# Attention and two feed-forward stages on one core: 1 / row sum spread through a four-row tile that a DMA makes, and the first chunk's sums copied by two engines in turn

## The chip, the core and the metric

The kernel runs on one core of a Trainium2 chip. The core has five engines that each work through their own instructions in order: TensorE (PE, matmuls; PEld in the profile is its loading of stationary operands), VectorE (DVE), ScalarE (ACT), GpSimd (POOL) and SyncE (SP). SP computes nothing here: it issues every DMA of this kernel, one after another, each when its inputs are ready. Engines wait for each other through semaphores. The metric is device time in microseconds, the median of the runs of one kernel.

## What is computed

The reference, cut to its arithmetic (q, k and v hold 2 x 8 heads of 768 x 64; 16 centroids per head; everything is float32):

```python
mask = argmax(q_n . c_n) == argmax(k_n . c_n)          # per head, cluster of each row
scores = where(mask, q @ k.T / sqrt(64), -1e9)
attn = exp(scores - max(scores))
attn = attn / (sum(attn) + 1e-9)
x = (attn @ v)  as [1536, 512]
x = square(relu(x @ w_in)) @ w_out                     # w_in 512 x 2048
p = domain_probs / (sum(domain_probs) + 1e-9)          # 4 experts
out = sum over e of p[:, e] * (relu(x @ w1[e]) @ w2[e])  # w1[e] 512 x 1024
```

## The kernel before

A float32 product is made of three products of float32r parts (high x high, high x low, low x high), so most values exist as a pair such as `hh`, `hl`.

**Attention** is a loop over 96 steps `g` (`NU`: 16 heads of 6 tiles of 128 query rows). In a step the kernel emits the scores of tile g+2 (`emit_S`, tile `s`), their maximum (`emit_max`, DVE), the exponential of tile g+1 with its row sums into `sums` (`emit_exp`, ACT), the transposes of tile g (`emit_T`: PE writes `t`, ACT copies it to `pth`, DVE makes `ptl`), and in turn one half of the product with v for two tiles (`emit_PV`, six matmuls, tile `po`). The table `ORDER` fixes the order inside even and odd steps. Two places of a step, `X1` and `X2`, take work from lists by step: PE's part stands there, and its copy out of PSUM (`Y1`, `Y2`) later in the step. `X1` takes the first piece of the step and `X2` the second. All these pieces share one PSUM buffer, `m` (`ps_m`, one buffer). Such pieces are the transposes of the next heads' k and q (`trans_slot`), the cluster products (`assign_slot`), the transposes of the one-hot cluster rows `oh` (`onehot_slot`, copied to `ohm` by ACT and sent by four DMAs), and the slots of `norm_slots`.

**norm_slots** divides by the row sums, once for each of 8 pairs of heads, numbered 0 to 7 here. After the last `emit_PO` of a pair its slots go into the list `nq`, one for each following step (`None` is a step without a piece). `f1` makes 1 / sum and splits it into two parts, `rs`. `f2` transposes `rs` by a matmul into `m`, ACT copies it to `rt` (24 rows of 128), and POOL adds `xm` to `xs`. `f3(0)` and `f3(1)` spread the values over 128 rows with a constant `sel` of ones and zeros, three matmuls of 128 columns each; ACT copies the result to `rb`, and POOL multiplies by `xs` and splits into `xh`, `xl`. For pair j, `f2` stands in step 12j+17. In step 12j+16 SP is given the loads of the next heads (`load_v`, `load_pair`: `nv`, `nk`, `nq`) and, late in the loop, of pieces of `w_out` (`load_piece`, tile `raw`).

**The last pair** (7) is emitted after the loop, written out by hand: `f1`, a first group of matmuls of the next stage (`early_gemm1(0)`), `f2`, the last products with v, `f3(0)`, `early_gemm1(1)`, `f3(1)`, `early_gemm1(2)` and so on; here ACT and DVE do POOL's part of `f3`.

**The two feed-forward stages** are one loop over 12 chunks `ci` of 512 hidden columns, 3 blocks `tb` of 512 tokens and 4 groups `m` of 128 columns. A step of it emits `gemm1` (12 matmuls, then ACT's relu, square and cast, POOL's `hl`), then the `gemm2` of four steps before (12 matmuls into four PSUM tiles `o0` to `o3`, one buffer each) and then `run_plan`, the splitting of later weights (ACT casts `w0h` or `w1h`, and DVE makes the low part, then five operations on `cva` for the next block). When a block's sum over a chunk is complete, `evac` takes `o0` to `o3` to `acc`: for the first chunk by four ACT copies (line 682), later by DVE adds (line 684).

Of the kernel before, what the change touches and what calls it, by code (L numbers as in the profile page):

```python
# [8 lines left out]
F32 = mybir.dt.float32  # L9
F32R = mybir.dt.float32r  # L10
I32 = mybir.dt.int32
AF = mybir.ActivationFunctionType
ALU = mybir.AluOpType
# [20 lines left out]
def moe_attention_kernel(  # L34
# [13 lines left out]
    nc = tc.nc  # L48
# [5 lines left out]
    B, H, S, D = q.shape  # L54
# [3 lines left out]
    NTT = S // 128  # L58
# [4 lines left out]
    HALF = S // 2  # L63
    QT = HALF // 128
# [5 lines left out]
    const = ctx.enter_context(tc.tile_pool(name="const", bufs=1))  # L70
# [5 lines left out]
    identf = const.tile([128, 128], F32, name="identf")  # L76
    identr = const.tile([128, 128], F32R, name="identr")
    zeros = const.tile([128, 1, 1], F32, name="zeros")
    cc = const.tile([128, H, 2 * C], F32R, name="cc")
    wgt = const.tile([128, 1, C], F32, name="wgt")  # L80
    sel = const.tile([NTT * 4, NTT, 128], F32R, name="sel")
    pe_p = const.tile([128, B * NTT, E], F32, name="pe_p")

    xh = [xpool.tile([128, KD, TB], F32R, name=f"xh{i}") for i in range(NTB)]
# [126 lines left out]
    with tc.manual_schedule():  # L211
# [8 lines left out]
        xs_p = right(actx, "xs", 2)  # L220
        sm_p = right(actx, "sm", 4)
# [53 lines left out]
            nc.gpsimd.memset(wgt[:, :, c:c + 1], float(C - c))  # L275


        idv = identf[0:NTT * 4, 0:NTT * 4].rearrange("p (t h s) -> p t h s", t=NTT, h=2)
        for h in range(2):
            nc.vector.tensor_tensor(  # L280
                sel[:, :, h * D:(h + 1) * D],
                idv[:, :, h, 0:1].to_broadcast([NTT * 4, NTT, D]),
                idv[:, :, h, 1:2].to_broadcast([NTT * 4, NTT, D]), op=ALU.add)

# [283 lines left out]
        def norm_slots(hp, last=False):  # L570
            st = {}
            def f1():
                sm = sums_t.pop(hp)
                r = sm_p.tile([128, 2, NTT], F32, tag="r", name="r", bufs=1)
                rs = st["rs"] = sm_p.tile([128, NTT, 2, 2], F32R, tag="rs", name="rs", bufs=2)
                rv = r.rearrange("p h t -> p t h")
                dq.extend([
                    lambda: nc.vector.tensor_scalar(r, sm, 1e-9, None, op0=ALU.add),
                    lambda: nc.vector.reciprocal(r, r),
                    lambda: nc.vector.tensor_copy(rs[:, :, :, 0], rv),  # L580
                    lambda: nc.vector.tensor_tensor(
                        rs[:, :, :, 1], rv, rs[:, :, :, 0].bitcast(F32), op=ALU.subtract),
                ])

            def f2():
                m = ps_m.tile([NTT * 4, 128], F32R, tag="m", name="m")
                nc.tensor.transpose(m, st["rs"].rearrange("p t h s -> p (t h s)"), identr)

                def evac():
                    rt = st["rt"] = xs_p.tile([NTT * 4, 128], F32R, tag="rt", name="rt")  # L590
                    nc.scalar.copy(rt, m.bitcast(F32))
                    if hp in xm_t:
                        xm = xm_t.pop(hp)
                        nc.gpsimd.tensor_tensor(xs_t[hp], xs_t[hp], xm, op=ALU.add)
                return evac

            def f3(half):
                b, kt = divmod(hp, H // 2)
                m = ps_m.tile([128, HALF], F32, tag="m", name="m")
                for j in range(QT):  # L600
                    nc.tensor.matmul(  # L601
                        m[:, j * 128:(j + 1) * 128], sel[:, half * QT + j], st["rt"],
                        start=True, stop=True)

                def evac():
                    rb = xs_p.tile([128, HALF], F32, tag="rb", name="rb")
                    nc.scalar.copy(rb, m)
                    (nc.vector if last else nc.gpsimd).tensor_tensor(
                        rb, rb, xs_t[hp][:, half * HALF:(half + 1) * HALF], op=ALU.mult)
                    c0 = b * S + half * HALF  # L610
                    col = c0
                    while col < c0 + HALF:
                        tb, o = divmod(col, TB)
                        n = min(TB - o, c0 + HALF - col)
                        xn = rb[:, col - c0:col - c0 + n]
                        hi = xh[tb][:, kt, o:o + n]
                        if last:
                            nc.scalar.copy(hi, xn)
                        else:
                            round_pool(hi, xn)  # L620
                        (nc.vector if last else nc.gpsimd).tensor_tensor(
                            xl[tb][:, kt, o:o + n], xn, hi.bitcast(F32), op=ALU.subtract)
                        col += n
                return evac

            return [f1, None, None, f2, lambda: f3(0), lambda: f3(1)]


        mp = {}
# [2 lines left out]
        o_t = {}  # L632
# [43 lines left out]
        def evac(ci, tb, n):  # L676
            first = ci in (0, NC1)
            last = ci in (NC1 - 1, NCH - 1)
            acc = acc_t[tb][:, n]
            if ci < NC1:  # L680
                if first:
                    nc.scalar.copy(acc, o_t[n])
                else:
                    nc.vector.tensor_tensor(acc, o_t[n], acc, op=ALU.add)
                if last:
# [228 lines left out]
            gemm1(*its[n], ps=s[:, 0])  # L914

        hp, pr = NH // 2 - 1, NU // 2 - 1
        f1, _, _, f2, f3, f4 = norm_slots(hp, last=True)
        f1()
        while dq:
            dq.pop(0)()  # L920
# [70 lines left out]
```

## Time and profile before

| | us |
|---|---|
| median of 2 runs | 1083.69 (1083.56 to 1083.82) |
| the profiled execution's own time | 1085.59 |
| its span, first to last instruction | 1083.8 |
| PE busy | 1055.2 (97%) |
| DVE busy | 503.8 (46%) |
| ACT busy | 431.0 (40%) |
| POOL busy | 326.3 (30%) |

Times in rows are microseconds from the span's start; "L601" is line 601 of the kernel before. A timeline row gives start, duration, engine, line, operation, written tile <- read tiles, shape, count, and in brackets how long the engine had been idle and what it waited for. Matmuls overlap in PE's pipeline, so the distance between two starts tells more than a matmul's duration. A DMA's row on SP is the time that SP spends issuing it; "to landing" counts from the start of the issue until the data is there. PEclk is the granted clock of PE as a share of full speed.

### The profile page before, as it was taken

The page shows a single profiled execution, that of the slowest core. Times are in us where ns is not written, and L with a number is a line of the kernel's source. Part 1 is how long each engine was busy: PE and PEld are TensorE (multiplying, and loading weights), DVE is VectorE, ACT ScalarE, POOL GpSimd, SP SyncE. Part 2 cuts the span into 40 slices and gives each one's busy share as a digit, 9 for nine tenths or more (in the row PEclk, how much of TensorE's full clock was granted, in tenths as well). Part 3 has the DMA queues.
Part 4 walks back from the last instruction along what each step waited for, and adds up shares of the span by engine and source line. Part 5 has one row for each costly group of instructions (what it writes and reads, how often), then busy time and mean ns, then how long its engine had stood idle before and what let it go on. Part 6 is the DMA issues. An engine that isn't in the chain of part 4 may idle for free.

```text
span 1083.8 us, 14176 instructions
## 1 busy us (share of the span) xinstructions
PE 1055.2 (97%) x5457; PEld 901.4 (83%) x5457; DVE 503.8 (46%) x838; ACT 431.0 (40%) x879; POOL 326.3 (30%) x405
## 2 busy tenths in 40 slices
PE   8899999998999999999999999999999999999998
PEld 7889888998887888888888888888888888888886
DVE  8688888787788763821122222222222223222322
ACT  6588887887655543434432121211212111121110
POOL 2457766665222222224534020211202112020000
PEclk9899999999999999999999999999999999999999
DMA  5666666873023230211102011110111102000012
GB/s 153 157 152 141 151 153 159 202 177 93 1 78 117 81 114 10 107 39 39 40 1 78 1 39 39 39 39 1 39 39 40 39 1 78 0 1 1 1 39 78
DMA packets 56978, 74.73 MB, mean 69 GB/s; under 512 B 26576, under 2 KB 32016, under 8 KB 56912
## 3 DMA queue, kind: packets, MB, share of 16 engines
q1 hardware_dynamic: 56912, 73.84, 25.0%
q8 instruction: 43, 0.70, 0.3%
q14 instruction: 23, 0.19, 0.1%
HBM read 43.05 MB, written 3.15 MB: 43 GB/s over the span
## 4 chain that ended last, share of the span: by engine, by line
PE 76%; DVE 3%; ACT 1%; DMA 1%; POOL 1%; issue 1%; SPq 0%; POOLq 0%; ACTq 0%
PE o L671 35%; PE h L641 11%; PE h L643 11%; PE h L642 11%; PE t L522 2%; PE s L489 2%; PE po L538 1%; PE po L536 1%; DVE cva L173 1%; PE m L388 1%; DMA q<-nql 1%; DVE cva L178 0%; PE m L601 0%; ACT p L509 0%; DMA k<-nkh 0%
## 5 line engine op out<-in xcount | busy, mean ns | idle before, releaser
L655 DVE SCALAR_TENSOR_TENSOR hl<-h,hh 128x512 fp32r<-128x512 f32 x96 | 66.4, 692 | 393.4 <-ACT hh L654 393.4
L654 ACT ACTIVATE hh<-h 128x512 fp32r<-128x512 f32 x96 | 57.4, 598 | 429.0 <-PE h L643 429.0
L641 PE MATMUL h<-xh,w0h 128*128 128x512 f32 x560 | 218.0, 389 | 0.0
L642 PE MATMUL h<-xl,w0h 128*128 128x512 f32 x560 | 217.9, 389 | 0.0
L643 PE MATMUL h<-xh,w0l 128*128 128x512 f32 x560 | 217.8, 389 | 0.0
L671 PE MATMUL o<-w1h,hh 128*128 128x512 f32 x384 | 149.4, 389 | 0.0
L671 PE MATMUL o<-w1l,hh 128*128 128x512 f32 x384 | 149.4, 389 | 0.0
L671 PE MATMUL o<-w1h,hl 128*128 128x512 f32 x384 | 149.4, 389 | 0.0
L643 PEld LDWEIGHTS h<-xh,w0l 128*128 128x128 f32 x560 | 105.2, 188 | 22.0
L641 PEld LDWEIGHTS h<-xh,w0h 128*128 128x128 f32 x560 | 105.3, 188 | 21.8
L642 PEld LDWEIGHTS h<-xl,w0h 128*128 128x128 f32 x560 | 105.1, 188 | 21.9
L652 POOL TENSOR_TENSOR hl<-r,hh 128x512 fp32r<-128x512 f32 x48 | 63.3, 1318 | 186.4 <-ACT hh L651 125.0
L528 DVE TENSOR_TENSOR ptl<-t,pth 128x384 fp32r<-128x384 f32 x192 | 99.3, 551 | 28.9 <-ACT pth L527 28.5
L196 POOL TENSOR_TENSOR w0l<-raw,w0h 128x512 fp32r<-128x512 f32 x32 | 41.2, 1289 | 236.7 <-ACT w0h L195 236.7
L498 DVE TENSOR_REDUCE nb<-s 128x1 f32<-128x768 f32 x96 | 91.2, 950 | 16.8 <-PE s L489 15.6
L527 ACT CAST pth<-t 128x384 fp32r<-128x384 f32 x192 | 83.2, 485 | 28.4 <-PE t L522 27.8
L522 PE MATMUL t<-identf,p 128*128 128x128 f32 x576 | 88.1, 280 | 6.2 <-DVE ptl L528 6.0
L489 PE MATMUL s<-k,q 80*128 80x384 f32 (+1 forms) x384 | 87.4, 348 | 3.1 <-DMA k<-ohm 2.7
L509 ACT ACTIVATE p<-s,nb 128x768 f32<-128x768 f32 x96 | 87.4, 911 | 7.0 <-DVE nb L498 6.9
L671 PEld LDWEIGHTS o<-w1l,hh 128*128 128x128 f32 x384 | 72.1, 188 | 15.0
L671 PEld LDWEIGHTS o<-w1h,hh 128*128 128x128 f32 x384 | 72.0, 188 | 15.0
L671 PEld LDWEIGHTS o<-w1h,hl 128*128 128x128 f32 x384 | 72.0, 188 | 15.0
(154 smaller groups left out, 1627.1 us busy)
## 6 DMA issues: line engine op xcount, KB each, us to landing
raw<-in_moe_w_dram SPq DMA_DIRECT2D x16, 1024.0 KB, 5.1
raw<-in_moe_w_in_dram SPq DMA_DIRECT2D x8, 1024.0 KB, 5.1
q<-nqh SPq DMA_DIRECT2D x42, 192.0 KB, 3.0
raw<-in_moe_w_out_dram SPq DMA_DIRECT2D x6, 1024.0 KB, 5.0
k<-nkh SPq DMA_DIRECT2D x28, 192.0 KB, 3.3
q<-nql SPq DMA_DIRECT2D x28, 192.0 KB, 3.8
nv<-in_v_dram SPq DMA_DIRECT2D x16, 192.0 KB, 3.7
out_dram<-acc SPq DMA_DIRECT2D x12, 256.0 KB, 2.1
```

Source lines behind the costliest of these rows:

```text
L489: nc.tensor.matmul(s[:, j, 0:HALF], stk[i, nq][:, t * 128:(t + 1) * 128], stk[i, nk][:, j * HALF:(j + 1) * HALF], start=first, stop=not first)
L498: nc.vector.tensor_reduce(out=nb, in_=s_ps[u][:, :, 0:HALF], axis=AX.XY, op=ALU.max, negate=True)
L509: nc.scalar.activation(p, s_ps.pop(u)[:, :, 0:HALF], AF.Exp, bias=nb_t.pop(u), accum_out=sums_t[hp][:, i % 2, t:t + 1])
L522: nc.tensor.transpose(tp[:, j], p_sb[u][:, half, j * 128:(j + 1) * 128], identf)
L527: return (lambda: nc.scalar.copy(dh, tp), lambda: nc.vector.tensor_tensor(dl, tp, dh.bitcast(F32), op=ALU.subtract))
L528: lambda: nc.vector.tensor_tensor(dl, tp, dh.bitcast(F32), op=ALU.subtract))
L641: nc.tensor.matmul(ps, wh[:, kt, ms], xh[tb][:, kt], start=(kt == 0), stop=False)
L642: nc.tensor.matmul(ps, wh[:, kt, ms], xl[tb][:, kt], start=False, stop=False)
L643: nc.tensor.matmul(ps, wl[:, kt, ms], xh[tb][:, kt], start=False, stop=(kt == KD - 1))
L652: nc.gpsimd.tensor_tensor(hl, r, hh.bitcast(F32), op=ALU.subtract)
L655: nc.vector.scalar_tensor_tensor(out=hl, in0=ps, scalar=0.0, in1=hh.bitcast(F32), op0=ALU.max, op1=ALU.subtract)
L671: nc.tensor.matmul(o_t[n], a, b, start=(ft == 0 and z == 0), stop=(ft == NF - 1 and z == 2))
```

## The change

Two edits.

**1 / sum.** `rs` is laid out with the tile index last, so the transposed `rt` has its 24 rows in the order (head, part, tile). Behind ACT's copy a new DMA on SP turns `rt` into `rw`, 4 rows (head, part) of 768 columns. `sel` shrinks to 4 x 128, and each `f3` is one matmul of 384 columns that reads `rw`. The slots get one more `None`, so `f3(0)` and `f3(1)` move one step later. After the loop, pair 7 keeps its order.

**First chunk's sums.** `o0` and `o2` are still copied by ACT, `o1` and `o3` now by DVE.

```diff
-    sel = const.tile([NTT * 4, NTT, 128], F32R, name="sel")
+    sel = const.tile([4, 128], F32R, name="sel")
...
-                rs = st["rs"] = sm_p.tile([128, NTT, 2, 2], F32R, tag="rs", name="rs", bufs=2)
-                rv = r.rearrange("p h t -> p t h")
+                rs = st["rs"] = sm_p.tile([128, 2, 2, NTT], F32R, tag="rs", name="rs", bufs=2)
+                rv = r
...
                     nc.scalar.copy(rt, m.bitcast(F32))
+                    rw = st["rw"] = xs_p.tile([4, S], F32R, tag="rw", name="rw", bufs=1)
+                    nc.sync.dma_start(
+                        out=rw.bitcast(F32).rearrange("c (t n) -> c t n", t=NTT),
+                        in_=rt.bitcast(F32))
...
-                for j in range(QT):
-                    nc.tensor.matmul(
-                        m[:, j * 128:(j + 1) * 128], sel[:, half * QT + j], st["rt"],
-                        start=True, stop=True)
+                nc.tensor.matmul(
+                    m, sel, st["rw"][:, half * HALF:(half + 1) * HALF], start=True, stop=True)
...
-            return [f1, None, None, f2, lambda: f3(0), lambda: f3(1)]
+            return [f1, None, None, f2, None, lambda: f3(0), lambda: f3(1)]
...
                 if first:
-                    nc.scalar.copy(acc, o_t[n])
+                    if n % 2:
+                        nc.vector.tensor_copy(acc, o_t[n])
+                    else:
+                        nc.scalar.copy(acc, o_t[n])
...
-        f1, _, _, f2, f3, f4 = norm_slots(hp, last=True)
+        f1, _, _, f2, _, f3, f4 = norm_slots(hp, last=True)
```

Where the new DMA stands on SP, first as it was around the normalisation of pair 0 (`nv`, `nk`, `nq` are the loads of later heads, `k` and `q` the stacked operands of a coming head):

```order
L248 DMA nv<-in_v_dram 128x384
L241 DMA nk<-in_k_dram 128x6x64 x2
L241 DMA nq<-in_q_dram 128x6x64 x2
L379 DMA k_1282<-nkh 64x768
L381 DMA k_1282<-nkl 64x768
L379 DMA q_1285<-nqh 64x768
```

and as it is with the change (lines of the changed kernel):

```order
L248 DMA nv<-in_v_dram 128x384
L241 DMA nk<-in_k_dram 128x6x64 x2
L241 DMA nq<-in_q_dram 128x6x64 x2
L592 DMA rw<-rt 4x6x128
L378 DMA k_1271<-nkh 64x768
L380 DMA k_1271<-nkl 64x768
L378 DMA q_1274<-nqh 64x768
```

The DMA stands behind the loads of `nv`, `nk`, `nq` and ahead of the next `k`; for pair 4 two `raw` pieces of 256 KB stand between `nq` and it as well, for pair 5 two such pieces and no `nk`, `nq`, and for pairs 6 and 7 nothing near.

On PE, steps 18 to 20 around the same place before (`t` the transposes, `po` the products with v, `m<-rt,sel` the two `f3`, `m<-identr,oh` the transposes of one-hot rows):

```order
L522 MATMUL t<-identf,p 128x128 x3
L601 MATMUL m<-rt,sel 128x128 x3
L522 MATMUL t<-identf,p 128x128 x3
...
L601 MATMUL m<-rt,sel 128x128 x3
L522 MATMUL t<-identf,p 128x128 x6
...
L448 MATMUL m<-identr,oh 64x128 x3
L522 MATMUL t<-identf,p 128x128 x3
L536 MATMUL po<-pth,vv 128x256
```

and with the change:

```order
L488 MATMUL s<-k_1390,q_1392 128x384 x2
L603 MATMUL m<-rw,sel 128x384
L521 MATMUL t<-identf,p 128x128 x6
...
L447 MATMUL m<-identr,oh 64x128 x3
L521 MATMUL t<-identf,p 128x128 x3
L603 MATMUL m<-rw,sel 128x384
L535 MATMUL po<-pth,vv 128x256
```

`f3(0)` now has the place in step 19 that `f3(1)` had, and `f3(1)` stands in step 20 as a second piece, behind the one-hot transposes, which write the same single buffer `m`.

On DVE, where the first block's sum of the first chunk is taken over, before (one round of weight splitting, and the next):

```order
L173 SCALAR_TENSOR_TENSOR cva<-raw,cva 128x512
L178 SCALAR_TENSOR_TENSOR cva<-raw,cva 128x512
L186 TENSOR_TENSOR w0l<-cva,w0h 128x4x128
L162 TENSOR_SCALAR cva<-raw 128x512
L165 TENSOR_SCALAR cva<-cva 128x512
```

and with the change:

```order
L173 SCALAR_TENSOR_TENSOR cva<-raw,cva 128x512
L178 SCALAR_TENSOR_TENSOR cva<-raw,cva 128x512
L684 COPY acc_4768<-o_4795 128x512
L684 COPY acc_4768<-o_4803 128x512
L186 TENSOR_TENSOR w0l<-cva,w0h 128x4x128
L162 TENSOR_SCALAR cva<-raw 128x512
```

The copies of `o1` and `o3` stand on DVE behind the whole round of splitting that `run_plan` gave it a step before.

## Rows read from the trace of the kernel before

**Rows 1.** Windows of the span by stage: attention, the passage from attention to the feed-forward stages, and the steady feed-forward stages. Columns: length, then busy time and count of PE, PEld, DVE, ACT and POOL, granted clock of PE, share of the DMA engines, GB/s.

```profile
60.00:120.00 60.00, 56.19 (x434) 52.62 (x433) 53.13 (x95) 47.87 (x115) 39.35 (x62) 1.00 0.67 151
300.00:360.00 60.00, 57.80 (x248) 47.37 (x247) 50.87 (x76) 32.02 (x56) 15.27 (x12) 0.97 0.29 91
600.00:800.00 200.00, 200.00 (x884) 165.59 (x883) 48.60 (x72) 33.98 (x61) 30.91 (x24) 1.00 0.10 32
```

**Rows 2.** Timeline of PE, steps 17 to 19 (normalisation of pair 0).

```profile
72.09 0.87 PE L489 MATMUL s<-k,q 128*128 128x384 f32 x4
...
74.23 0.87 PE L489 MATMUL s<-k,q 128*128 128x384 f32 x4
76.45 0.55 PE L522 MATMUL t<-identf,p 128*128 128x128 f32 x3 [1.35 <-DVE ptl L528]
76.93 0.55 PE L601 MATMUL m<-rt,sel 24*128 24x128 f32 x3
...
78.50 0.87 PE L489 MATMUL s<-k,q 128*128 128x384 f32 x4
79.29 0.55 PE L601 MATMUL m<-rt,sel 24*128 24x128 f32 x3
79.77 0.87 PE L522 MATMUL t<-identf,p 128*128 128x128 f32 x6
```

**Rows 3.** Timeline of ACT and SP at the same place: the copy that makes `rt`, the issue of two `nq` loads, the issue after them.

```profile
73.06 0.25 ACT L591 CAST rt<-m 24x128 fp32r<-24x128 f32 x1
...
74.60 2.43 SPq L241 DMA_DIRECT2D nq<-in_q_dram  x2
...
77.07 0.77 SPq L379 DMA_DIRECT2D k<-nkh  x1
```

**Rows 4.** The view of one tile's instructions, for the second of those `nq` loads (issue in ns, its start, then its time to landing) and for the `k` behind it (its time to landing).

```profile
L241 SPq DMA_DIRECT2D nq<-in_q_dram x1: 1739/1739/1739, 75.3 to 75.3; - x1
DMA to landing us min/median/max: 5.1/5.1/5.1
...
DMA to landing us min/median/max: 3.6/3.6/3.6
```

**Rows 5.** The same for pair 4 (PE's `f3(1)`; the `raw` piece that the new DMA will follow and its time to landing) and for pair 5 (the same, two pieces in one answer).

```profile
211.92 0.55 PE L601 MATMUL m<-rt,sel 24*128 24x128 f32 x3
L105 SPq DMA_DIRECT2D raw<-in_moe_w_out_dram x1: 431/431/431, 211.0 to 211.0; - x1
DMA to landing us min/median/max: 5.2/5.2/5.2
244.69 0.55 PE L601 MATMUL m<-rt,sel 24*128 24x128 f32 x3
L105 SPq DMA_DIRECT2D raw<-in_moe_w_out_dram x2: 447/708/969, 239.4 to 240.4; - x2
DMA to landing us min/median/max: 4.7/4.9/5.1
```

**Rows 6.** All 60 DMAs from `ohm` (24 KB each), the view of that tile: time to landing. Then the timeline of step 20 after pair 0: the one-hot transposes into `m`, ACT's copy of it, and PE's next product.

```profile
DMA to landing us min/median/max: 1.9/1.9/3.9
...
82.30 0.37 PE L448 MATMUL m<-identr,oh 128*64 128x128 f32 x3
82.71 0.47 ACT L453 CAST ohm<-m 64x384 fp32r<-64x384 f32 x1
82.77 0.37 PE L536 MATMUL po<-pth,vv 128*128 128x256 f32 x1
```

**Rows 7.** Timeline of PE after pair 4: two waits that the kernel before has there.

```profile
215.36 0.38 PE L448 MATMUL m<-identr,oh 128*64 128x128 f32 x3 [0.34 <-POOL oh L422]
218.16 0.81 PE L388 MATMUL m<-cc,k 128*128 128x32 f32 x6 [0.68 <-DMA k<-nkl]
```

**Rows 8.** Timeline of the last pair (7), after the loop: `rt`, `f3(0)`, the relu after `early_gemm1(1)`, and DVE's part of `f3(1)`.

```profile
293.33 0.25 ACT L591 CAST rt<-m 24x128 fp32r<-24x128 f32 x1
293.63 0.55 PE L601 MATMUL m<-rt,sel 24*128 24x128 f32 x3 [0.62 <-ACT rt L591]
...
297.17 0.60 ACT L649 ACTIVATE r<-s 128x512 f32<-128x512 f32 x1 [1.20 <-PE s L643]
...
299.50 1.37 DVE L608 TENSOR_TENSOR rb<-rb,xs 128x384 f32<-128x384 f32 x1 [3.06 <-ACT rb L607]
```

**Rows 9.** Timeline where the first block's sum is taken over: the end of a `gemm1`, ACT's four copies, PE's wait for the first of them, and the last of DVE's five operations of that round. Then the group of DVE's later adds from the same PSUM tiles, from the view of lines by form (count, then busy us, mean ns).

```profile
327.38 0.39 PE L643 MATMUL h<-xh,w0l 128*128 128x512 f32 x1
329.33 2.04 ACT L682 COPY acc<-o 128x512 f32<-128x512 f32 x4
329.96 0.50 PE L671 MATMUL o<-hh,w1h 128*128 128x512 f32 x1 [2.20 <-ACT acc L682]
331.41 0.69 DVE L178 SCALAR_TENSOR_TENSOR cva<-raw,cva 128x512 int32<-128x512 int32 x1
...
L684 DVE TENSOR_TENSOR acc<-o,acc 128x512 f32<-128x512 f32 x36 | 23.6, 687 | 83.2 <-PE o L671 83.2
```

**Rows 10.** PE around two long waits: a wait in the attention loop, and windows of PE alone (length, busy time and count, granted clock) that begin with the end of it and with the end of the wait of rows 9.

```profile
269.20 0.58 PE L489 MATMUL s<-k,q 80*128 80x384 f32 x2 [2.69 <-DMA k<-ohm]
269.00:274.00 5.00, 4.80 (x26) 0.66 0.00 0
331.00:335.00 4.00, 4.00 (x12) 0.57 0.06 25
```

More of the change, by code (lines that the diff above doesn't have):

```diff
@@ L275, in moe_attention_kernel @@
             nc.gpsimd.memset(wgt[:, :, c:c + 1], float(C - c))
-        idv = identf[0:NTT * 4, 0:NTT * 4].rearrange("p (t h s) -> p t h s", t=NTT, h=2)
+        idv = identf[0:4, 0:4].rearrange("p (h s) -> p h s", s=2)
         for h in range(2):
             nc.vector.tensor_tensor(
-                sel[:, :, h * D:(h + 1) * D],
-                idv[:, :, h, 0:1].to_broadcast([NTT * 4, NTT, D]),
-                idv[:, :, h, 1:2].to_broadcast([NTT * 4, NTT, D]), op=ALU.add)
+                sel[:, h * D:(h + 1) * D], idv[:, h, 0:1].to_broadcast([4, D]),
+                idv[:, h, 1:2].to_broadcast([4, D]), op=ALU.add)
         vt, stk, kq, ohs = {}, {}, {}, {}
@@ L579, in f1 @@
                     lambda: nc.vector.reciprocal(r, r),
-                    lambda: nc.vector.tensor_copy(rs[:, :, :, 0], rv),
+                    lambda: nc.vector.tensor_copy(rs[:, :, 0], rv),
                     lambda: nc.vector.tensor_tensor(
-                        rs[:, :, :, 1], rv, rs[:, :, :, 0].bitcast(F32), op=ALU.subtract),
+                        rs[:, :, 1], rv, rs[:, :, 0].bitcast(F32), op=ALU.subtract),
                 ])
@@ L586, in f2 @@
                 m = ps_m.tile([NTT * 4, 128], F32R, tag="m", name="m")
-                nc.tensor.transpose(m, st["rs"].rearrange("p t h s -> p (t h s)"), identr)
+                nc.tensor.transpose(m, st["rs"].rearrange("p h s t -> p (h s t)"), identr)
                 def evac():
```

## The prediction, made before the changed kernel ran

> **What bounds the kernel now.** I first read the busy times by stage [rows 1]. In the feed-forward stages PE is busy for all of 200 us, 884 matmuls, 0.226 us each, and no other engine reaches a quarter of that. Nothing that the change touches later than the first chunk can matter there, and every microsecond by which PE enters this stretch late stays to the end. In the attention loop PE is busy for 56.2 of 60 us and DVE for 53.1, so I read a step of PE in the timeline. One step takes 74.23 - 72.09 = 2.14 us [rows 2] and is filled with matmuls that start one behind the other; PE paces the loop, and its few waits are written in brackets. A new wait of PE there is therefore added to the time, unless one of the old waits shrinks by it. The third place is the passage at 290 to 335 us. There PE waits 0.62 us for `rt` [rows 8] and 2.20 us for ACT's copy of `o0` [rows 9]. What is late behind the second wait is DVE and ACT: their chain of weight splitting starts at DVE's `rb` of `f3(1)`, for which DVE has waited 3.06 us, because ACT's `rb` stands behind the relu of a `gemm1` that itself waited 1.20 us for PE [rows 8]. So a delay of PE at `f3(0)` is carried into DVE's chain, and cannot be caught up there.
>
> **Fewer matmuls.** Three matmuls of `f3` hold PE from 79.29 to 79.77, 0.48 us. Four of the same 384 columns as the new one take 78.50 to 79.29, 0.20 each [rows 2]. The change saves 0.28 us, 16 times: -4.5. `f3(0)` also leaves step 18, so PE comes to its new place, that of the old `f3(1)`, 0.48 us earlier than before.
>
> **The new DMA in the attention loop.** `rt` is done at 73.31, but in SP's order the DMA stands behind two `nq` loads, whose issue ends at 77.03 [rows 3]. It starts where `k<-nkh` now starts, at 77.07. The price of its landing is not in the trace, so I bound it. Lower bound: it lands as an unhindered small DMA does, 1.9 us after its issue [rows 6], at 79.0. Upper bound: it lands with the `k` behind it, at 77.07 + 3.6 = 80.7. Between them lies the landing of the `nq` just ahead, 75.3 + 5.1 = 80.4 [rows 4]. I take that one: loads issued at about 0.7 us apart are landing 5 us after their issue, so there is a backlog, and a later DMA should get through about when the one ahead of it does. PE wants the data at 79.29 - 0.48 = 78.8. Pair 0 waits 1.6 us (bounds 0.2 and 1.9). For pair 4 the `raw` piece ahead lands at 211.0 + 5.2 = 216.2, and PE is there at 211.92 - 0.48 = 211.4: 4.8 us (lower bound 211.0 + 0.4 + 1.9 - 211.4 = 1.9). For pair 5 it is 240.4 + 5.1 = 245.5 against 244.2: 1.3 us (lower bound 0) [rows 5]. Pairs 1 to 3 have the order of pair 0; I take the mean of pairs 0 and 5 for each, 1.45. For pair 6 no load is near, and two steps of 2.14 us cover 1.9 us. Sum: 1.6 + 4.35 + 4.8 + 1.3 = 12.1, between 2.5 and about 14.
>
> What is queued behind the waiting matmul on PE is the rest of step 19, transposes and products, on which ACT and DVE live; they idle too. The issues behind it on SP start some 0.6 us later, and their heads are needed steps later.
>
> **The shared buffer.** `f3(1)` is now a second piece in step 20, behind the one-hot transposes, and both write the one buffer `m`. ACT has copied that buffer at 82.71 + 0.47 = 83.18, while PE is ready at 82.77 [rows 6]: 0.4 us of waiting, for the six pairs that have such a step, +2.4. In return POOL's products for `f3(0)` no longer stand ahead of the one-hot operations, and after pair 4 two old waits, 0.34 for POOL and 0.68 for a DMA [rows 7], end while PE waits for the new DMA: -1.0.
>
> **The last pair.** Nothing but the DMA stands between `rt`, done at 293.58, and `f3(0)`, which started at 293.63 [rows 8]. SP is free, so the small DMA's 1.9 us [rows 6] are paid in full: +1.9. They go through `f3(0)` to `gemm1`, relu and DVE, as said above.
>
> **The first chunk's copies.** ACT's copy of `o0` is not changed, so PE still resumes at 329.96. Its next tile is `o1`, three matmuls of 0.226 later, at 330.64. DVE's copy of `o1` stands behind the five operations of its round, the last of which ends at 331.41 + 0.69 = 332.10 [rows 9]; a copy by DVE is priced as its add from the same tiles, 0.69 us. PE gets `o1` at 332.8, 2.2 us late. `o3` follows at 333.5 and is wanted no sooner than 334.2. Lower bound: the new wait covers part of a stretch that ran at the lower clock before, 1.4 us; upper bound 3.8, if another such stretch follows. I take 2.2. For the later two blocks I found no wait of PE for these copies to shorten, and ACT's gain of two copies there is time that nobody waits for.
>
> **The clock.** After waits of 2.69 and 2.20 us the granted clock fell to half: 0.66 over 5 us and 0.57 over 4 us [rows 10], each 1.7 us of PE lost. After the wait of 1.35 us at 76.45 [rows 2] it did not: 1.00 over that stage [rows 1]. The new waits of pair 4 (4.8) and of the last pair (0.62 + 1.9) are above 2.2, so I add 1.7 twice, +3.4. Those of the other pairs lie nearer to 1.35, and I add nothing for them.
>
> **The sum.** -4.5 + 12.1 + 2.4 - 1.0 + 1.9 + 2.2 + 3.4 = +16.5. The profiled execution took 1085.6 in all, 1.8 of it outside its span, and would take 1102.1; the median of the runs shown is 1.9 below it, 1083.7, and would be 1100.2. I predict 1100, slower by 1.5%. A measurement of this kernel can tell about 2% from no change, so by that measure this is the same time.
>
> **Rivals.** *The DMA is not held up.* If small DMAs overtake the backlog, the waits sum to 2.5 and not 12.1, and the fall of the clock after pair 4 is in doubt: 1100.2 - 9.6 - 1.7 = 1089. Against it speaks that 60 small DMAs of `ohm` took up to 3.9 us [rows 6]; for it, that their median is 1.9. [...]
>
> *The clock falls after every wait.* In pairs 0 to 3 the new wait follows 2.4 us behind the old one of 1.35 us. If five more waits (pairs 0 to 3 and 5) cost 1.7 each, 1100.2 + 8.5 = 1109, slower by 2.3%. It decides from the third such fall on: 1083.7 x 1.02 = 1105.4 is 5.2 above my sum. For it: the waits of pairs 0 to 3 come to about 3 us in two parts. Against it: no wait of up to 1.35 us did this in 60 to 120 us. [...]
>
> *The waits are hidden and the matmuls win.* If DVE's lag (53 of 60 us) is what really paces attention, PE's new waits shorten others: -4.5 + 1.9 + 1.7 + 2.2 = about +1, 1085. Against it stand PE's unbroken steps [rows 2]. A gain of over 2% would need 22 us, and the change removes 4.5.
>
> **Chances.** My sum, 1094 to 1105, has 0.52; the overtaking DMA 0.20; the clock after every wait, or the upper bounds together, 0.20; hidden waits 0.08. Leaving out 2 in 10 gives a range of 1088 to 1109. Faster by over 2% 0.01, within 2% 0.79, slower by over 2% 0.20.
>
> **What would show it.** In the changed profile PE's matmul `m<-rw` should have waits named after a DMA in pairs 0 to 5, the longest in pair 4 at 4 to 5 us, none in pair 6, one of about 2 us in the last pair; the second matmul of a pair should wait some 0.4 us for ACT's copy of `ohm`; PE should wait twice at the first `gemm2` behind the first block, for ACT and then about 2 us for DVE. The granted clock of the windows at pair 4 and the last pair should drop. I am wrong if the DMA lands 2 us after its issue at pair 0, or if the attention loop does not grow by what PE waits.

## The result and the profile after

The changed kernel takes 1096.46 us (1096.41 to 1096.51, two runs) against 1083.69 us before (two runs), 12.8 us more. The ratio on record, which is not simply that of the two medians, is 1.0114 with a 95% interval of 1.0092 to 1.0136: about 1.1% slower, clear of no change, and inside the 2% below which two times of this kernel count as the same. The forecast was 1100, with a range of 1088 to 1109. The profiled execution took 1096.41 us, with a span of 1094.6 us. It lies at the changed kernel's median, while the profiled execution of before lies 1.9 us above the median of before; so the spans differ by 10.8 us only. Of the executions behind this document, three far off the rest (2702 us of e1, its profiled one, 1311 us of e5 and 1761 us of the kernel before) count in no ratio.

To see where the time went I take the same matmul in both traces and ask how much later it starts. This distance is +0.3 us at 70 us of the trace of before and +10.9 from 337 us on; behind that it does not change. It grows by 4.4 us in attention, 3.5 in the last pair and 2.6 where the first chunk's sums are taken over.

The windows by stage, which answer to [rows 1]: PE lost 2.1 us of busy time in 60 to 120, and the granted clock fell from 0.97 to 0.91 in 300 to 360. The steady stage is what it was.

```profile
60.00:120.00 60.00, 54.12 (x408) 49.72 (x407) 53.72 (x93) 48.06 (x114) 37.42 (x58) 1.00 0.68 151
300.00:360.00 60.00, 55.82 (x223) 44.51 (x224) 45.79 (x71) 27.59 (x49) 12.88 (x10) 0.91 0.27 88
600.00:800.00 200.00, 200.00 (x885) 165.64 (x884) 51.08 (x76) 34.02 (x61) 31.94 (x25) 1.00 0.10 35
```

The view of one tile, `rw`, on PE in the changed kernel (duration in ns: least, median, most; then for what PE sat idle ahead of these matmuls, in us and times):

```profile
L603 PE MATMUL m<-rw,sel x16: 432/438/684, 80.6 to 305.5; 4*128 4x384 f32 x16
its engine sat idle before it (us, times) until:
  DMA rw<-rt: 11.8, 7
  ACT ohm L452: 1.4, 6
```

Seven waits for the DMA and six for ACT's copy of `ohm`, as the prediction listed them. The timelines of pair 0 (ACT, SP, then PE with both halves), which answer to [rows 2, 3]:

```profile
73.42 0.26 ACT L590 CAST rt<-m 24x128 fp32r<-24x128 f32 x1
...
74.95 3.08 SPq L241 DMA_DIRECT2D nq<-in_q_dram  x2
78.14 0.79 SPq L592 DMA_DIRECT2D rw<-rt  x1
...
80.59 0.44 PE L603 MATMUL m<-rw,sel 4*128 4x384 f32 x1 [1.36 <-DMA rw<-rt]
80.96 0.77 PE L521 MATMUL t<-identf,p 128*128 128x128 f32 x5
...
83.61 0.49 PE L521 MATMUL t<-identf,p 128*128 128x128 f32 x3
84.33 0.44 PE L603 MATMUL m<-rw,sel 4*128 4x384 f32 x1 [0.23 <-ACT ohm L452]
```

`rt` is ready at 73.68. The DMA is issued 4.5 us later, when SP has issued the loads ahead of it, and the data are there 2.4 us after that. Two further readings: from the start of one product to that of the next matmul it is 80.96 - 80.59 = 0.37 us, not the 0.20 that I took; and in pairs 1 to 3 the waits are 0.87, 1.09 and 0.81. The wait for `ohm` costs more than its bracket: the product starts 84.33 - 83.61 = 0.72 us behind the transposes ahead of it. Before, the transposes at this place were

```profile
82.51 0.51 PE L522 MATMUL t<-identf,p 128*128 128x128 f32 x3
```

and the next product came 82.77 - 82.51 = 0.26 us behind them [rows 6]. So the wait costs 0.46 us from start to start, of which PE shows 0.23 as idle.

Pair 4, which answers to [rows 5], has SP, PE, and a window of PE behind the wait (length, busy time, granted clock):

```profile
212.88 1.59 SPq L105 DMA_DIRECT2D raw<-in_moe_w_out_dram  x2
214.57 0.75 SPq L592 DMA_DIRECT2D rw<-rt  x1
...
218.92 0.68 PE L603 MATMUL m<-rw,sel 4*128 4x384 f32 x1 [4.50 <-DMA rw<-rt]
...
218.90:222.30 3.40, 3.38 (x14) 0.50 0.42 100
```

This is the long wait forecast, with a stretch of 3.4 us at a granted clock of 0.50 behind it, which costs half of it, 1.7 us. The last pair, which answers to [rows 8], and its window:

```profile
298.11 0.25 ACT L590 CAST rt<-m 24x128 fp32r<-24x128 f32 x1
298.39 0.65 SPq L592 DMA_DIRECT2D rw<-rt  x1
...
300.61 0.47 PE L603 MATMUL m<-rw,sel 4*128 4x384 f32 x1 [2.82 <-DMA rw<-rt]
...
300.80:304.20 3.40, 3.40 (x9) 0.50 0.00 0
```

Here SP is free and the DMA is issued 0.03 us after `rt`; the 2.2 us from there to the product are what this DMA took with no other near it on SP. In the window behind it matmuls of 512 columns start 0.43 us apart, and after the window 0.23. And the first chunk's copies, PE, DVE and two windows of PE, which answer to [rows 9, 10]:

```profile
338.36 0.79 PE L672 MATMUL o<-hh,w1h 128*128 128x512 f32 x1 [2.30 <-ACT acc L686]
341.27 0.79 PE L672 MATMUL o<-hh,w1h 128*128 128x512 f32 x1 [1.27 <-DVE acc L684]
...
339.80 0.69 DVE L178 SCALAR_TENSOR_TENSOR cva<-raw,cva 128x512 int32<-128x512 int32 x1
340.53 1.29 DVE L684 COPY acc<-o 128x512 f32<-128x512 f32 x2
...
338.40:341.80 3.40, 2.13 (x4) 0.50 0.38 154
341.80:345.20 3.40, 3.40 (x9) 0.50 0.00 0
```

DVE's copies stand behind the round of splitting. PE waits 1.27 us more, and the stretch at 0.50 is twice as long as before, 6.8 us.

### The profile page after: what moved, and what is told of

The parts are those of the page before. It is cut to its first block, busy times and chain, and to the rows that moved or that the text cites. A ratio compares the mean times of both kernels' runs of the same rounds, so it can differ in the third digit from the quotient of the medians.

```text
span 1094.6 us, 14122 instructions
## 1 busy us (share of the span) xinstructions
PE 1057.2 (97%) x5425; PEld 900.0 (82%) x5425; DVE 513.1 (47%) x844; ACT 429.3 (39%) x873; POOL 325.0 (30%) x405
## 4 chain that ended last, share of the span: by engine, by line
PE 83%; DVE 7%; SPq 3%; DMA 3%; ACT 3%; issue 1%; POOL 1%; ACTq 0%; POOLq 0%; DVEq 0%
PE o L672 35%; PE h L643 11%; PE h L644 11%; PE h L642 11%; PE t L521 3%; PE s L488 3%; PE po L535 2%; PE po L537 2%; PE m L387 2%; ACT p L508 1%; DVE ptl L527 1%; DMA rw<-rt 1%; DMA q<-nql 1%; DVE nb L497 1%; DVE cva L173 1%
```

## The experiments

Theory at this point: the loss is made of the waits for `rw` (in attention because its issue stands behind loads on SP, in the last pair because of the DMA's own time), the falls of the clock that two of them bring, and DVE's copies behind its splitting. The rivals are that the backlog of data and not SP's order is to blame, or that what the waits take would be given back anyway. The before-kernel's runs spread by some 8 us, so times are compared by the ratios on record, each with its 95% interval and taken against runs of the kernel before from the same round on the same chip (a ratio of two medians can differ from them by up to 0.0013, as in e1). "By the ratio" means the ratio times 1083.69 us. For the place of a gain I use the growth of PE's distance to the profile of before, in us. It is read from one profile each, so a fall of the clock that comes in one execution and not in another is in it; and it leaves out what lies ahead of 70 us, where e2 and e6, the same program as before up to there, are already 1.6 and 2.5 us ahead. The columns therefore need not add up to the ratio.

```
kernel                              pairs 0-3  pair 4 to   last   first   ratio to before
                                    (70-208)   289 us      pair   chunk
changed kernel                        +2.7      +1.7      +3.5    +2.6    1.0114 (1.0092 to 1.0136)
ACT copies (e1)                                                           1.0066 (1.0042 to 1.0089)
before, DVE copies (e2)                0.0      -2.7       0.0    +2.7    1.0032 (1.0016 to 1.0048)
DMA on ACT's queue (e3)               -1.8      +0.8      +4.7    +3.2    1.0052 (1.0035 to 1.0069)
DMA ahead of loads (e4)               -1.8      -0.9      +3.5    +3.2    1.0039 (1.0021 to 1.0056)
last pair as before (e5)              +2.1      +2.0       0.0    +2.2    1.0084 (1.0061 to 1.0107)
before, slots one later (e6)          -1.0      +0.9       0.0     0.0    0.9978 (0.9962 to 0.9994)
three remedies (e7)                   -0.8      +0.5       0.0    -1.6    0.9972 (0.9957 to 0.9987)
e7, transpose earlier (e8)            -4.6      -2.2       0.0     0.0    0.9941 (0.9920 to 0.9963)
before, transpose earlier (e9)        -3.8      +0.2       0.0     0.0    0.9951 (0.9934 to 0.9967)
changed, transpose earlier (e10)     +12.6      -0.8      +3.5    +2.9    1.0129 (1.0090 to 1.0169)
before, addition earlier (e11)        -3.9      +0.3       0.0    -1.6    0.9960 (0.9941 to 0.9978)
e8 again (e12)                        -4.3      -1.4       0.0     0.0    0.9937 (0.9916 to 0.9958)
```

**e1: ScalarE's copies again.**

```diff
-                    if n % 2:
-                        nc.vector.tensor_copy(acc, o_t[n])
-                    else:
-                        nc.scalar.copy(acc, o_t[n])
+                    nc.scalar.copy(acc, o_t[n])
```

> The changed kernel with all four copies of the first chunk on ScalarE again (the second edit undone). Theory: VectorE's two copies stand behind the splitting of the weights and cost what the offset of TensorE grows by there, 10.86 - 8.3 = 2.6 us; the span goes from 1094.6 to about 1092 and the time from 1096.5 to about 1093.9. Rival: the weights' loads set the time from there on and the 2.6 us are lost anyway a little later (no change, within 0.5 us of 1096.5).

This kernel is read by its times alone. Its ratio is 0.0048 below that of the changed kernel, 5.2 us; both intervals taken together (the root of their half widths' squares is 0.0032) leave 1.7 to 8.7. The 2.6 us expected lie in that, the rival's nothing does not.

**e2: DVE's copies alone**, the same lines put into the kernel before.

> The kernel before with the second edit alone (copies of the odd tiles on VectorE). Theory: + 2.2 to 2.6 us, time 1086 to 1086.5. Rival: the cost in the changed kernel came from the later start of the stage there and not from the copies; then the time stays at 1083.7. Together with the kernel with ScalarE's copies this tells whether the two edits add up.

Ratio 1.0032, 3.5 us (1.7 to 5.2, in which the 2.2 to 2.6 expected lie): the copies cost by themselves. PE in the trace of e2:

```profile
325.69 0.50 PE L671 MATMUL o<-hh,w1h 128*128 128x512 f32 x1 [2.20 <-ACT acc L685]
...
328.61 0.79 PE L671 MATMUL o<-hh,w1h 128*128 128x512 f32 x1 [1.77 <-DVE acc L683]
...
329.10:332.50 3.40, 3.40 (x9) 0.50 0.01 2
```

The first wait is that of before; the second is new, and the clock is at 0.50 for a stretch of 3.4 us more behind it. Together they give the +2.7 of the table, and e1 and e2 add up (0.0066 + 0.0032) to most of the whole, 0.0114.

**e3: the DMA on ScalarE's queue.**

```diff
-                    nc.sync.dma_start(
+                    nc.scalar.dma_start(
                         out=rw.bitcast(F32).rearrange("c (t n) -> c t n", t=NTT),
```

> The changed kernel with the DMA from rt to rw issued from ScalarE's queue instead of SyncE's; nothing else. Theory: in attention the tile is late because its issue stands behind the issues of the loads (issue 4.5, 2.4, 4.0 us after rt was written in pairs 0, 1, 4). Issued right behind rt it lands 3 to 4 us later, before or at the first matmul of the pairs, so that the waits of 0.8 to 4.5 us fall to under 1 us each, with the clock fall of pair 4; ScalarE pays the issue, up to 0.7 us a pair. The last pair keeps its wait of 2.8. Time 1089 to 1093. [...] Rival 2: what the waits take is given back by the waits behind them, so that without them the time falls by under 2 us (1095 to 1096.5).

1089.3 us by the ratio, as the theory said. ACT issues 0.03 us after `rt`, and pairs 0 to 4 have no wait. In pair 5 there is one of 1.49 us, 5.7 us after the issue at 238.17, although nothing on ACT's queue stood ahead of it. SP was issuing two `raw` pieces just then (237.21 to 238.65), and in e4, where they come behind it, that pair has no wait: the backlog of data, the first of the two rivals named above, looks right for this one pair.

**e4: the DMA ahead of the loads on SP.**

```diff
-... "load": -8,
+... "load": -6,
...
-                elif not cq and g % NTT == 4:
+                elif not cq and g % NTT == 0:
```

> The changed kernel with the loads of k and q two steps later (and the raw pieces of the weights two steps later), so that on SyncE's queue the DMA to rw stands ahead of them and is issued right behind rt; no other engine's order changes. Theory (the order of issues on SyncE decides): waits in pairs 0 to 3 and 5 under 0.5 us, pair 4's 4.5 us to under 1.5 us and its fall of the clock gone; time 1089 to 1093. Rival 1: given back by later waits, 1095 to 1096.5. Rival 2: the later loads hold up the transposes of the next heads' k and q, and new waits of 1 us or more appear there; 1095 or more.

1087.9 us, 1 us better than the theory's range. Only the loads' place differs from the changed kernel: two steps later, behind the DMA on SP. ACT, SP and PE at pair 0, and PE at pair 4:

```profile
74.74 0.26 ACT L590 CAST rt<-m 24x128 fp32r<-24x128 f32 x1
75.02 0.79 SPq L592 DMA_DIRECT2D rw<-rt  x1
...
80.53 0.43 PE L603 MATMUL m<-rw,sel 4*128 4x384 f32 x1
...
211.24 0.44 PE L603 MATMUL m<-rw,sel 4*128 4x384 f32 x1
```

No bracket, no wait: the issue is 0.02 us behind `rt`, and of the seven waits the last pair's alone is left. So the place of the issue among the loads makes the waits, and it does so in two ways that e4 takes away together. In the changed kernel SP issues the DMA 2.4 to 4.5 us behind `rt` in pairs 0 to 4; and in pairs 1 to 4, behind loads in flight, the data come 4.0 to 4.4 us after the issue, where the last pair needs 2.2. In pairs 1 to 3 either delay alone is longer than the wait; no run parts them there. In pairs 0 to 3 the waits were not given back either: they go from +2.7 to -1.8, more than the 4.1 us of their waits. Pair 4 loses its wait of 4.50 us, but two new ones of 0.65 and 0.55 us for `k` and `q` stand a little later, and the fall of the clock that was to be gone is still there. This is not rival 2: in e3 and in e6 below, whose loads are not moved, PE waits for the same `k` and `q` (0.54 and 0.98 us, and 1.57 us) and the clock falls there too. A PE that is early at pair 4 meets these waits, so rival 1 has a share in this one pair.

**e5: the last pair as before**, three matmuls a half from `rt` with a second table `sel3` of 24 rows.

```diff
...
+                if last:
+                    for j in range(QT):
+                        nc.tensor.matmul(
+                            m[:, j * 128:(j + 1) * 128], sel3[:, half * QT + j], st["rt"],
+                            start=True, stop=True)
+                else:
+                    nc.tensor.matmul(
+                        m, sel, st["rw"][:, half * HALF:(half + 1) * HALF], start=True, stop=True)
...
```

> The changed kernel, but the last pair (which has nothing left beside it) makes its two halves as before, three matmuls each from rt with a table of 24 rows, without the DMA; pairs 0 to 6 as changed. Theory: the last pair's wait goes from 2.82 back to 0.6 us and the fall of the clock behind it is gone; TensorE's offset to the kernel before, which grew by 3.5 us there (4.8 to 8.3), does not grow there: time about 3.5 us below the changed kernel's, ratio to before 1.008 +- 0.002. Rival: the early products of the next stage that follow are held up by the exponentials' engines anyway and half of it or more is lost again: 0 to 1.7 us gained.

The ratio is 1.0084 where 1.008 was expected. By the times alone this is not clear of no gain (0.0030 below the changed kernel, with a half width of 0.0032 for the two intervals together). The trace shows it: PE's distance does not grow at all there, the wait is back at 0.62 us, no fall follows, and nothing of the 3.5 us is lost again up to the first chunk's copies.

**e6: the slots alone.**

```diff
-            return [f1, None, None, f2, lambda: f3(0), lambda: f3(1)]
+            return [f1, None, None, f2, None, lambda: f3(0), lambda: f3(1)]
...
```

> The kernel before with one empty slot more ahead of the two halves, as the change has it; three matmuls a half from rt, no DMA, copies as before. Theory: the second half then stands behind the transposes of the next one-hot tile and waits 0.2 us (0.75 us in the offset) for the shared buffer m in each pair, 6 x 0.75 = 4.5 us, and the work that moves out of the step before lets the one-hot waits on GpSimd (4 x 0.6 to 1.0 us) vanish: the net is -1 to +2 us, ratio 0.999 to 1.002. Rival: the one-hot waits vanished in the changed kernel only because its TensorE came later (the DMA waits); then they stay here, and the time is 3 to 4.5 us above the kernel before, ratio 1.003 to 1.004.

Ratio 0.9978: the kernel before gets faster by 2.4 us (0.7 to 4.1) from one empty slot. PE at the one-hot transposes after pair 0, in the kernel before, then in e6:

```profile
98.97 0.37 PE L448 MATMUL m<-identr,oh 128*64 128x128 f32 x3 [0.99 <-POOL oh L422]
```

```profile
95.83 0.55 PE L522 MATMUL t<-identf,p 128*128 128x128 f32 x3
96.14 0.43 PE L448 MATMUL m<-identr,oh 128*64 128x128 f32 x3
```

The wait for GpSimd is gone, and so are the three like it (0.99, 0.99 and 0.58 us). That PE is earlier here in span time says little, since 2.5 us of it were there at 70 us. Counted from that point, GpSimd's last operation on `oh` ends 0.7 us sooner than before (at 95.76 us, against 98.91 before) and PE is ready for it 0.6 us later (at 96.14, against 97.98), so both have a part. The rival, that the changed kernel lost these waits only by its waits for the DMA, falls, since e6 has none. The extra slot of the change is a gain and not a cost, by its times; its own profile shows 0.1 us of it only, -1.0 and then +0.9 with a fall of the clock behind the wait of 1.57 us for `q` at 216.03.

**e7: three remedies together**, e4's order on SP, e5's last pair and e1's copies.

> All three remedies together: the DMA to rw ahead of the loads on SyncE's queue, the last pair without the DMA, all four copies on ScalarE. What is left of the change is one product per half in pairs 0 to 6 from the tile of four rows. Theory: attention gains 2 to 5 us against the kernel before (12 or 14 matmuls fewer of 0.28 us, and the waits on the one-hot tiles absorbed), the last pair and the first chunk cost what they did before: ratio 0.995 to 0.999. Rival: the falls of the clock that come with later loads, and waits that take the place of those removed, use it up: ratio 1.000 to 1.003.

Ratio 0.9972, in the theory's range: without its three faults the change wins 3 us (1.4 to 4.7). But e6, which has the slot alone, wins 2.4 of them, so this run does not show that the single product wins anything. The -1.6 in the first chunk is no part of that; it is a fall of the clock that did not happen in this execution (below).

**e8: the transpose one step earlier**, the halves where the kernel before has them.

```diff
-            return [f1, None, None, f2, None, lambda: f3(0), lambda: f3(1)]
+            return [f1, None, f2, None, lambda: f3(0), lambda: f3(1)]
...
```

> As the kernel with all three remedies, and the transpose of the reciprocals (with the DMA behind it) one step earlier, the two halves at the steps at which the kernel before has them. Theory: the tile of four rows has the same time to land, and the second half stands ahead of the one-hot transposes again, so that the wait for the shared buffer m goes (0.75 us in the offset in each of six pairs): ratio 0.002 to 0.004 below that of the kernel with the three remedies. Rival: the reciprocals on VectorE are not ready one step earlier, and TensorE waits 0.5 us or more for them in each pair, or the one-hot waits on GpSimd come back (4 x 1.0): no gain.

Ratio 0.9941, 0.0031 below e7 (0.0005 to 0.0057): the size was forecast, but not for my reason. The wait for `m` is gone (0.23 us of idling, six times), but the waits for GpSimd at the one-hot tiles are back (1.00, 0.41, 0.41 and 0.78 us), and PE's wait of 1.35 us for `ptl` [rows 2] has vanished in pairs 0 to 3, which I had not expected.

**e9: the kernel before with the transpose one step earlier**, to part the product from the move (`[f1, None, f2, None, f3(0), f3(1)]`, three matmuls from `rt`).

> The kernel before with the transpose of the reciprocals one step earlier and the halves where they are; three matmuls a half from rt, no DMA, copies as before. It differs from the kernel with all remedies and the earlier transpose (ratio 0.9941) in the product and its DMA alone. Theory: one product for three saves 2 x 0.28 us a pair in seven pairs, 3.9 us, so this one stands that much above it: ratio 0.997 to 0.9995. Rival: the gain came from the moved transpose and the product with its DMA is worth nothing: ratio 0.993 to 0.995.

Ratio 0.9951, at the edge of the rival's range and clear of the theory's. Nearly all of e8's gain is the moved step and not the product. The two kernels differ in one thing more than the expectation says: e8 also has the loads two steps later.

**e10: the changed kernel with the transpose one step earlier and the loads still ahead.**

```diff
-            return [f1, None, None, f2, None, lambda: f3(0), lambda: f3(1)]
+            return [f1, None, f2, None, None, lambda: f3(0), lambda: f3(1)]
...
```

> The changed kernel with the transpose of the reciprocals one step earlier, the halves where the change has them, and the loads of k and q still ahead of the DMA to rw on SyncE's queue (only in pair 4 the two raw pieces come to stand behind it). Theory: the issue is held up by the issues ahead of it and not by rt, so that rt's earlier time brings nothing in pairs 0 to 3: waits of 0.8 to 1.4 us again; in pair 4 the wait falls from 4.5 us by the 1.6 us of the raw pieces' issues. Time 1.5 to 3 us below the changed kernel's, ratio to before 1.008 to 1.010. Rival: the tile is late because rt is written late; then with a step more (2 to 3 us) the waits of pairs 0 to 3 go, and pair 4's falls under 2 us: ratio 1.004 to 1.006.

Both missed: 1097.7 us by the ratio (1.0129, 1.0090 to 1.0169). SP and PE in pair 1, then windows of PE behind the waits of pairs 0 to 3:

```profile
109.72 1.45 SPq L241 DMA_DIRECT2D nq<-in_q_dram  x2
111.27 1.19 SPq L592 DMA_DIRECT2D rw<-rt  x1
...
115.58 0.44 PE L603 MATMUL m<-rw,sel 4*128 4x384 f32 x1 [2.50 <-DMA rw<-rt]
...
80.00:84.00 4.00, 4.00 (x21) 0.62 0.50 108
116.00:120.00 4.00, 4.00 (x25) 0.65 0.66 141
152.00:156.00 4.00, 4.00 (x16) 0.50 0.28 65
190.00:194.00 4.00, 4.00 (x17) 0.50 0.14 32
```

The mechanism is the theory's: `rt` is a step earlier and the issue is not, it comes 4.0 to 4.3 us behind `rt` in pairs 0 to 4. But the waits grow to 1.95, 2.50, 3.16 and 3.13 us. In pairs 1 to 3 PE, free of its wait for `ptl`, arrives 1.3 to 1.4 us earlier after the issue than in the changed kernel; and the data come later after it, by 1.3 us in pair 0 and 0.2, 0.8 and 1.0 in pairs 1 to 3, for which I have no cause. In this profile the clock now falls behind each of them. That is the prediction's rival of the falling clock, in a kernel whose waits are 1.95 to 3.16 us. Not every execution need have all these falls: the six take 1090.71 to 1105.18 us with mean granted clocks of 0.993 to 0.976, and the profiled one, 1103.54, is the second slowest.

**e11: GpSimd's addition alone**, in the kernel before. `f2` issues `xs += xm` on GpSimd; here a slot `f0` of its own does so one step earlier and `f2` keeps its place (`[f1, None, f0, f2, f3(0), f3(1)]`).

> The kernel before with GpSimd's addition xs += xm one slot ahead of the transpose of the reciprocals; the transpose, the halves and everything else as they are. Theory from the traces: in the kernel before a splitting instruction on VectorE takes 2.28 us beside this addition (0.69 elsewhere), which holds TensorE up by 1.35 to 1.4 us in each of pairs 0 to 3; the gain of the kernels with the earlier transpose is this addition's move. Then this one gains as much as the kernel before with the earlier transpose: ratio 0.994 to 0.997, and the 1.4 us waits of the transposes of p for ptl are gone. Rival: the gain is the transpose's own place; ratio 0.999 to 1.001 and the waits stay.

Ratio 0.9960, and pairs 0 to 3 gain 3.9 us, as in e9. In the kernel before, GpSimd and DVE at step 17:

```profile
72.68 1.83 POOL L594 TENSOR_TENSOR xs<-xs,xm 128x768 f32<-128x768 f32 x1
72.78 2.28 DVE L178 SCALAR_TENSOR_TENSOR cva<-raw,cva 128x512 int32<-128x512 int32 x1
```

In e11, the same two, and the small cast that now meets the addition:

```profile
66.17 1.83 POOL L597 TENSOR_TENSOR xs<-xs,xm 128x768 f32<-128x768 f32 x1 [1.92 <-DMA xm<-xo]
67.23 0.81 DVE L580 CAST rs<-r 128x12 fp32r<-128x12 f32 x1
71.01 0.67 DVE L178 SCALAR_TENSOR_TENSOR cva<-raw,cva 128x512 int32<-128x512 int32 x1
```

The splitting instruction that took 2.28 us beside the addition takes 0.67 away from it, and with that PE's wait of [rows 2] goes. The theory holds.

**e12: e8 once more**, on the chip of e11.

> The kernel with all remedies and the earlier transpose once more, on the same chip as the one above. Theory: the product for three matmuls is worth under 0.56 us a pair, since part of it is given back at the one-hot waits: ratio 0.993 to 0.996, and 0 to 0.003 below the kernel with the addition moved. Rival: it is worth the full 3.9 us (0.0036).

Ratio 0.9937, e8's again. e8 and e12 are the fastest kernels of this study, 6 to 7 us below the kernel before. Of that, e9 and e11 have 4 to 5 us without the product; what the product adds, together with the later loads, is 0.0010 and 0.0023. Half widths of 0.0027 and 0.0028 part neither from nothing, nor from the 0.0036 of the rival. Against the rival stand e7 and e6, the same slots with and without the product and the later loads (0.0006, with a half width of 0.0022), and the traces: in pairs 0 to 3 they give the product 0.4 to 0.8 us.

## Why the prediction was right

The time fell inside the range and the verdict was the likeliest one, 3.5 us below the number. The terms, added up against spans, said +16.5 where +10.9 came. That the number missed by 3.5 us and the sum by 5.6 is luck: the forecast took off 1.9 us because the profile of before lies above its median, and the profile of the changed kernel does not. The terms:

- *Where it would be lost.* Right in all three places. The last pair: 1.9 + 1.7, less the two products, came to 3.0; measured 3.5, and e5 takes just that away. The copies: 2.2; measured 2.6 in the changed kernel and 2.7 in e2. It is only about half a wait; the rest is the longer stretch at 0.50, which I had kept for the upper bound.
- *The waits for the DMA.* Right in their cause (e4) and in pair 4 (4.8; measured 4.50, with the forecast fall of the clock). The choice that the DMA lands about with the load ahead of it held: in pair 0 the second `nq` lands 4.9 us after its issue at 75.6, and PE has `rw` at 80.59. But pairs 1 to 3 waited 0.92 us on average and not 1.45, and pair 5 0.36 and not 1.3. PE is not the cause: it is ready for the product (its start less its wait) 5.6 us behind `rt` in pairs 0 to 3 and 3.9 in pair 5, within 0.2 us of what I had taken. The loads ahead land sooner, 4.5 us after their issue in pairs 1 and 3 and 3.8 in pair 5, where I had read 5.1; and the mean of pairs 0 and 5 was no reading of pairs 1 to 3. The term was 12.1 and measured 1.36 + 0.87 + 1.09 + 0.81 + 4.50 + 0.36 = 9.0.
- *Fewer matmuls.* Mis-sized: 0.28 us a half was read from four matmuls of 384 columns in a row, 0.20 each [rows 2]. One by itself among others takes 0.37 from its start to the next, so that three matmuls of 0.48 give back 0.11. The term of -4.5 was worth -1.8 by starts; e7 against e6, 0.7 us (-1.7 to 3.0), fits that better than 4.5.
- *The slot.* The step that failed: "the shared buffer" was to cost 0.4 us in each of six pairs. The wait is there and of that size (0.46 us from start to start in pair 0, 0.23 of it idle), but the extra slot also ended GpSimd's waits at the one-hot tiles after pairs 0 to 3, 3.6 us in all. I had seen that GpSimd's products leave that place, and had not looked for the waits of PE for GpSimd behind it. e6 gives the whole move as -1.0 us over pairs 0 to 3, where the term has +1.6.
- *The end of attention.* Not foreseen: before, PE waits 2.69 us at 269.20 and the clock falls [rows 10]; in the changed kernel the same matmul, 275.74 us into the span, waits 0.93 us and the clock stays, 3.5 us less. Only a part of it belongs to the change. In e2 attention is the kernel before's, and there the wait is 1.92 with no fall behind it.
- *The clock.* Forecast as two falls, +3.4. The four windows above hold 13.6 us at 0.50, where the kernel before has two stretches of 3.4 [rows 10]: 3.4 us lost more, as forecast, but in part by luck. Three stretches are new, the one at the copies among them, and the one at the end of attention is gone.

These add up: for attention I had +11.3, and 2.4 (14 halves of 0.17 that are not saved) - 3.1 - 2.6 - 3.5 = -6.8 takes it to 4.5; measured +4.4. Two of these corrections are not the change's alone, the -2.6 being read from e6 and the -3.5 being in part one execution's. So the sum came near because misses of both signs met; the places, and the cause of the waits, are no luck.

Of the rivals, the overtaking DMA did not happen (the data came 4.0 to 4.4 us after the issue in pairs 1 to 4); the clock did not fall after the waits of 0.8 to 1.4 us for `rw`, and did after the longer ones in the profile of e10; and hidden waits were wrong as a whole, though the slot's gain is a piece of it. What stays open is the worth of the single product in time: by starts 1.8 us at most, by ratios 0.0006 to 0.0023, inside their intervals.

## What to carry to other kernels

A DMA that takes part of a row of dependent steps is priced from when its issue comes up on its queue (2.4 to 4.5 us behind `rt` in pairs 0 to 4 here, 0.02 us in pair 0 of e4); put it ahead of loads that nobody awaits, and keep it out of places where no other work covers its 2.2 us (the last pair here). A matmul by itself can cost more than one in a run of its like (0.37 us against 0.20 here), so replacing three small ones by one can save less than the columns say (0.11 us a half here, for the 0.28 expected). Before an extra slot is counted as a cost, look at what else shares the step it leaves.

## What the runs showed of the hardware

Beside GpSimd's addition of two SBUF tiles, two DVE instructions that read SBUF alone took longer. In the rows of the kernel before that stand under e11, the splitting on DVE begins at 72.78 us, the addition ends at 74.51, and the splitting ends at 75.06, 0.55 us behind it: 2.28 us, where 0.69 is the median of its line. In e11 the cast of 12 columns, 0.17 us in the kernel before, took 0.81 beside it, while a DVE reduction of the PSUM tile `m` took its usual 0.55.

The same is seen in the round of splitting ahead of DVE's copies, before as after: its line 173 takes 1.74 us beside GpSimd's `hl` (1.28 us before, 1.27 after), and 0.69 at its median. So 1.05 us of DVE's lateness at `o1` go with GpSimd's work; no run moves it.

The clock did not fall each time after a like wait, and it fell where no wait was long. PE at the one wait before the end of attention in e6, and a window behind it:

```profile
268.21 0.58 PE L489 MATMUL s<-k,q 80*128 80x384 f32 x2 [2.56 <-DMA k<-ohm]
...
268.00:272.00 4.00, 3.79 (x30) 1.00 0.00 0
```

and in e7 at the first chunk's copies:

```profile
326.56 0.50 PE L685 MATMUL o<-hh,w1h 128*128 128x512 f32 x1 [2.20 <-ACT acc L696]
...
326.00:330.00 4.00, 3.44 (x15) 1.00 0.50 204
330.00:334.00 4.00, 4.00 (x20) 1.00 0.00 0
```

After waits of 2.69 and 2.20 us at the same places the kernel before fell to 0.66 and 0.57 [rows 10], and 1.7 us were lost each time. At pair 4 the clock fell in e6, which has no DMA to `rw`, behind the wait of 1.57 us for `q`, and in e11 behind waits of 0.30, 0.26 and 0.20 us. The windows are e6's, then e11's, with all engines as in [rows 1]:

```profile
216.00:220.00 4.00, 3.97 (x19) 4.00 (x20) 2.02 (x4) 0.96 (x2) 2.22 (x4) 0.50 0.84 180
```

```profile
212.00:216.00 4.00, 3.80 (x23) 3.73 (x23) 2.29 (x5) 1.02 (x3) 2.68 (x5) 0.66 0.52 115
```

One profile thus shows a fall that the next execution may not have (e12's six had mean granted clocks of 0.995 to 1.000), and a difference of 1.7 us between two profiles says nothing until a second one has it too. I did not find what decides it.
